# Strassen's scheme for the second product of experts 4 to 7 in the first super chunk, with half of the T blocks of w1 split beside the gated product

## The chip, the cores and the metric

The program runs on one core of one Trainium2 chip. The metric is the device time of one execution in microseconds, taken as the median of the runs shown. Times of single instructions and waits come from one profiled execution.

## The reference

Three layers follow one another. Only the third is touched by the change.

```python
x = attn_out.transpose(0, 2, 1, 3).reshape(2304, 512)       # linear attention, 32 heads
x = ((x @ w1) * (x @ w2) @ w3) @ w_out                       # gated product
def _moe2_ref(x, w_gate, w1, w2):                            # 8 experts, D = 512, F = 1024
    P = ...                                                  # 8 Sinkhorn rounds over x @ w_gate
    out = np.zeros((N, D), dtype=np.float32)
    for e in range(E):
        h = np.maximum(x @ w1[e], 0.0)                       # first product
        ye = h @ w2[e]                                       # second product
        out += P[:, e:e + 1] * ye
    return out
```

## The kernel before, in words

Every fp32 operand of a matmul is held as a high and a low part. `copy` makes the high part on ScalarE (a cast, line 96) and `subtract` the low part on VectorE (line 99). A product is then three matmuls (`mm3`, lines 87 to 89: high by high, low by high, high by low).

The gated product runs from about 235 to 558 us in six blocks `j` of 384 tokens, each with 16 accumulations `ab` and 4 accumulations `px`; `ab` has four PSUM banks. Beside it run 48 jobs (`sum_load`, `sum_make`, `sum_next`). Two of three jobs form the four sums T1 to T4 of a block of moe2_w1 that Strassen's scheme needs and store them to `W1T`. The third forms the sums of a block of moe2_w2 for one of the experts in `EARLY` (0, 1, 2 and 7), splits them with `copy` and `subtract` and stores high and low part to `W2S`. A job's tile `tr` has three buffers and its tile `tt` two. The load for job n+3 is issued by `sum_make(n)` and waits until the buffer is free.

The third layer has three super chunks `s` of 768 tokens. A super chunk runs over 8 experts `e`, each of 4 units `p`, and a unit `u` is (s, e, p). The first product of a unit (`products`) is by Strassen's scheme in all three super chunks: seven products of 384 columns on the operands a11, s2, s3, s1, a22, a12 and s4, each in one PSUM bank, which `c` then collects on VectorE (line 836). The weights of units 0 to 31 are loaded in fp32 (`load_w1`), split (`prep_w1`) and stored to `W1S`. Later super chunks load them from there (`back_w1`).

After four units comes the second product of the expert. In super chunk 0 it is a plain product of 512 columns, `py` at line 942, and `split_w2` and `sums_w2` prepare the parts of w2 that the later super chunks read. In super chunks 1 and 2 it is Strassen's scheme again: the PSUM pool has seven banks, `operands` makes the operands a, b, d and e from `c`, and seven groups of 36 matmuls of 256 columns (lines 1039 to 1041) multiply them with the blocks K11, K21, KT4, KT1, KN2, K22 and KT3 of w2, in this order. `load_t` loads these blocks from `W2S` into a ring `tk` of three buffers. A block is named t*s*_*e*_*k*, with k from 0 to 6.

Before the last second product of a super chunk, `load_x` loads the x of the next one (`rx`) and `prep_x` makes its seven operands with sums in a scratch tile `xs`, which is a tile of the pool `rx`. All DMAs named here are issued by SyncE (SP), in the order of the program, and a DMA that has to wait holds up all behind it. A scheduler sets the order on each engine, starting from the order of the code and its priorities.

Of the kernel before, what the change touches and what calls it, by code (L numbers as in the profile page):

```python
# [27 lines left out]
def kernel(  # L28
# [17 lines left out]
    nc = tc.nc  # L46
# [51 lines left out]
    def subtract(key, out, a, b, i=0):  # L98
# [11 lines left out]
        [scr.tile([P, 2, n, 2 * P], F32, name=f"w1s{i}_{n}") for n in (2, 5)]  # L110
        for i in range(NE * FT2 // 2)
    ]
    DH = DM // 2
    W2S = [scr.tile([P, 7, FT2 // 2, 2, DH], F32, name=f"w2s{i}") for i in range(NE)]

    W1T = [scr.tile([P, 4, 2 * P], F32, name=f"w1t{i}") for i in range(NE * FT2 // 2)]
# [363 lines left out]
    def prep_x(s):  # L480
# [3 lines left out]
        t = rx.tile([P, 2, N1], F32, name=f"xs{s}", tag="s")  # L484
# [22 lines left out]

    def load_w1(u):
        if u < len(units):
            s, e, p = units[u]  # L510
            if s > 0:
                return
            rawW1[u] = rw1.tile([P, 7, 2 * P], F32, name=f"r1_{u}", tag="r")
            nc.sync.dma_start(rawW1[u][:, 4:7], moe2_w1[e, p][:, 1:4])
            nc.sync.dma_start(rawW1[u][:, 0:4], W1T[u])
# [39 lines left out]
    EARLY = (0, 1, 2, NE - 1)  # L555

    def w2_rows(e, p):
        return moe2_w2[e].rearrange("(j n p) (h d) -> n p j h d", j=2, p=P, h=2)[p]

    def make_t(e, p, t, hi):  # L560
# [5 lines left out]
        lo = t.bitcast(F32R)  # L566
        copy("Th", hi, t)
        subtract("Tl", lo, t, f32(hi))
        for i, x in enumerate((hi, lo)):
            nc.sync.dma_start(W2S[e][:, 0:4, p, i], f32(x))  # L570

    first_jobs = [("w1", k) for k in range(len(W1T))]
# [13 lines left out]
    def sum_make(n):  # L586
        kind, k = jobs[n]
        t = tq[0].tile([P, 4, 2 * P], F32R if kind == "w2" else F32, name=f"tt{n}", tag="tt")
        if kind == "w2":
            make_t(*k, rawT[n], t)  # L590
            sum_load(n + 3)
            return
        b12, b11, b21, b22 = (rawT[n][:, i] for i in range(4))
        t1, t2, t3, t4 = (t[:, i] for i in range(4))
        add("Wt", t1, b12, b11, ALU.subtract, k)
        add("Wt", t3, b22, b12, ALU.subtract, k)
        add("Wt", t2, b22, t1, ALU.subtract, k)
        add("Wt", t4, b21, t2, ALU.subtract, k)
        sum_load(n + 3)
        nc.sync.dma_start(W1T[k], t)  # L600
# [10 lines left out]
    with ExitStack() as c2:  # L611
# [81 lines left out]
        for j in range(NT // N1):  # L693
# [26 lines left out]
            if c0 + N1 == NT:  # L720
# [5 lines left out]
                wc1 = sbuf(c4, "wc1", 2, "left")  # L726
# [40 lines left out]
    with c4:  # L767
# [24 lines left out]
        def split_w2(u):  # L792
# [10 lines left out]
            if e in EARLY:  # L803
                load_w2(u + len(RW))
# [353 lines left out]
```

## Time and profile before

| | |
|---|---|
| median of 3 runs | 2020.35 us (2019.73 to 2021.43) |
| the profiled execution | 2020.68 us, span of its instructions 2018.9 us |
| TensorE (PE) busy | 1987.1 us, 98% |
| VectorE (DVE) busy | 1426.9 us, 71% |
| ScalarE (ACT) busy | 779.6 us, 39% |
| granted TensorE clock | 0.995 of full speed over the span |
| DMA | 496.78 MB, 246 GB/s in the mean |

Each line gives an engine's busy time in the profiled execution. Super chunk 0 lies at 557.9 to 1064.5 us, super chunk 1 at 1064.5 to 1541, super chunk 2 after that.

### The profile page before, as it was taken

How to read it: one execution, taken by the hardware profiler on the slowest of the kernel's cores; microseconds unless marked ns; L12 is line 12 of the kernel's file. 1: busy time of each engine (PE TensorE's matmuls, PEld its weight loads, DVE VectorE, ACT ScalarE, POOL GpSimd, SP SyncE). 2: the span in 40 equal slices, each digit the busy share in tenths (PEclk: the TensorE clock that was granted, in tenths of full speed). 3: DMA queues.
4: the chain of work that ended last, by engine and by line, in shares of the span. 5: the costliest groups of instructions: out<-in, count | busy, mean ns of one | idle time of the engine just before them, and what ended most of it. 6: DMA issues, size and time to landing. Idle time of an engine off the chain costs nothing.

```text
span 2018.9 us, 33841 instructions
## 1 busy us (share of the span) xinstructions
PE 1987.1 (98%) x13605; PEld 1867.6 (93%) x13605; DVE 1426.9 (71%) x2454; ACT 779.6 (39%) x1435; POOL 92.4 (5%) x126
## 2 busy tenths in 40 slices
PE   7899999999999999999999999999999999999999
PEld 6676789999998888998889999999999999999999
DVE  7766775666687558877776766677778667786666
ACT  6666532323443224433333333334334333433333
POOL 3433200000000000000000000000000000000000
PEclk9999999999999999999999999999999999999999
DMA  6443247888597668989977677666778677666674
GB/s 213 146 140 108 90 151 255 275 294 283 197 342 286 245 250 303 330 315 317 326 269 277 237 252 255 246 247 248 251 250 307 243 246 252 249 250 248 243 253 152
DMA packets 155501, 496.78 MB, mean 246 GB/s; under 512 B 12624, under 2 KB 73936, under 8 KB 128464
## 3 DMA queue, kind: packets, MB, share of 16 engines
q1 hardware_dynamic: 154752, 493.96, 69.3%
q8 instruction: 107, 1.75, 0.4%
q10 hardware_dynamic: 592, 0.66, 0.1%
q14 instruction: 50, 0.41, 0.1%
HBM read 348.82 MB, written 145.75 MB: 245 GB/s over the span
## 4 chain that ended last, share of the span: by engine, by line
PE 87%; DVE 5%; ACT 3%; POOL 2%; DMA 2%; issue 1%; SPq 0%; ACTq 0%; POOLq 0%; DVEq 0%
PE ps L87 6%; PE ps L89 6%; PE ps L88 6%; PE pa L87 5%; PE pa L89 5%; PE pa L88 5%; PE py L89 4%; PE py L88 4%; PE py L87 4%; PE b L1041 3%; PE b L1040 3%; PE b L1039 3%; PE ab L89 3%; PE ab L87 3%; PE ab L88 3%; PE a L1039 2%
## 5 line engine op out<-in xcount | busy, mean ns | idle before, releaser
L836 DVE TENSOR_TENSOR c<-c,ps 128x384 f32<-128x384 f32 x480 | 255.9, 549 | 58.5 <-PE ps L89 54.2
L834 ACT COPY c<-pa 128x384 f32<-128x384 f32 x96 | 45.7, 476 | 321.0 <-PE pa L89 278.4
L89 PE MATMUL py<-w,hL 128*128 128x512 f32 x384 | 152.1, 397 | 0.0
L88 PE MATMUL py<-w,hH 128*128 128x512 f32 x384 | 152.0, 397 | 0.0
L87 PE MATMUL py<-w,hH 128*128 128x512 f32 x384 | 151.2, 397 | 0.0
L1058 DVE SCALAR_TENSOR_TENSOR o<-mt,Pw,o 128x512 f32<-128x512 f32 x84 | 58.4, 749 | 122.5 <-ACT mt L1048 122.5
L89 PE MATMUL ab<-XH,wL 128*128 128x384 f32 x384 | 131.1, 341 | 1.4 <-DVE wL L99 1.4
L87 PE MATMUL ab<-XH,wH 128*128 128x384 f32 x384 | 131.0, 341 | 1.2 <-ACT wH L96 1.0
L88 PE MATMUL ab<-XL,wH 128*128 128x384 f32 x384 | 130.4, 339 | 0.0
L836 DVE TENSOR_TENSOR c<-c,pa 128x384 f32<-128x384 f32 x192 | 103.0, 549 | 10.0 <-PE pa L89 9.0
L1039 PE MATMUL b<-t,dh 128*128 128x256 f32 x384 | 108.7, 283 | 0.0
L1040 PE MATMUL b<-t,dh 128*128 128x256 f32 x384 | 108.7, 283 | 0.0
L1041 PE MATMUL b<-t,dl 128*128 128x256 f32 x384 | 108.7, 283 | 0.0
L958 DVE SCALAR_TENSOR_TENSOR o<-py,Pw,o 128x512 f32<-128x512 f32 x42 | 31.5, 750 | 109.1 <-PE py L89 108.8
L993 ACT ACTIVATE c<-c 128x384 f32<-128x384 f32 x64 | 33.7, 526 | 155.6 <-DVE c L836 155.6
L96 ACT CAST w<-r 128x1024 fp32r<-128x1024 f32 (+2 forms) x96 | 63.8, 690 | 71.7 <-PE pa L89 27.1
L87 PEld LDWEIGHTS py<-w,hH 128*128 128x128 f32 x384 | 72.3, 188 | 17.4 <-DVE o L958 0.3
L89 PEld LDWEIGHTS py<-w,hL 128*128 128x128 f32 x384 | 72.3, 188 | 17.3
L88 PEld LDWEIGHTS py<-w,hH 128*128 128x128 f32 x384 | 72.4, 188 | 17.1
L87 PEld LDWEIGHTS ab<-XH,wH 128*128 128x128 f32 x384 | 72.6, 189 | 2.9 <-ACT wH L96 1.3
L99 DVE TENSOR_TENSOR w<-r,w 128x512 fp32r<-128x512 f32 (+2 forms) x96 | 72.5, 774 | 3.2 <-ACT w L96 3.0
L89 PEld LDWEIGHTS ab<-XH,wL 128*128 128x128 f32 x384 | 72.5, 189 | 2.1 <-DVE wL L99 2.1
(259 smaller groups left out, 6306.1 us busy)
## 6 DMA issues: line engine op xcount, KB each, us to landing
t<-w2s SPq DMA_DIRECT2D x112, 1024.0 KB, 4.8
w<-w1s SPq DMA_DIRECT2D x64, 1280.0 KB, 5.5
w1s<-w SPq DMA_DIRECT2D x32, 1280.0 KB, 7.1
w<-w1s SPq DMA_DIRECT2D x64, 512.0 KB, 5.0
tr<-in_moe_w_dram SPq DMA_DIRECT2D x48, 512.0 KB, 5.2
w2s<-w SPq DMA_DIRECT2D x96, 256.0 KB, 4.3
w1t<-tt SPq DMA_DIRECT2D x32, 512.0 KB, 6.4
r<-w1t SPq DMA_DIRECT2D x32, 512.0 KB, 6.8
```

The lines of the kernel that those rows point to most:

```text
L87: nc.tensor.matmul(ps, aH, bH, start=start, stop=False)
L88: nc.tensor.matmul(ps, aH, bL, start=False, stop=False)
L89: return nc.tensor.matmul(ps, aL, bH, start=False, stop=stop).ins
L96: (e.copy if e is nc.scalar else e.tensor_copy)(out, src)
L99: engine(key, i).tensor_tensor(out, a, b, ALU.subtract)
L834: first[0] = nc.scalar.copy(o, ps).ins
L836: nc.vector.tensor_tensor(o, t, ps, ALU.add)
L993: nc.scalar.activation(c22, c22, AF.Relu)
L1039: nc.tensor.matmul(dst[i], H[:, c], T[:, 0], start=f, stop=False, skip_group_check=True)
L1040: nc.tensor.matmul(dst[i], H[:, c], T[:, 1], start=False, stop=False, skip_group_check=True)
L1041: nc.tensor.matmul(dst[i], L[:, c], T[:, 0], start=False, stop=l, skip_group_check=True)
L1058: nc.vector.scalar_tensor_tensor(o, src[i], w, o, ALU.mult, ALU.add)
```

## The change

Experts 4 to 7 of super chunk 0 (units 16 to 31; `NUC` is 16) now take the path of the later super chunks: `operands`, `load_t` and the seven groups. Experts 0 to 3 stay as they were. `EARLY` is now experts 4 to 7, so that the jobs beside the gated product prepare the sums of w2 for these, and `sums_w2` prepares those of experts 0 to 3 within super chunk 0. For experts 4 to 7 of super chunk 0 `load_t` reads the plain blocks K11, K21 and K22 in fp32 through a tile `kr` with one buffer, splits them and stores them to `W2S`.

The jobs that form T1 to T4 of w1 for units 16 to 31 now split them too and store high and low part to `W1S`. For these units `get_w1` loads the T blocks from `W1S` and splits only B11, B21 and B22, which come through a tile `rwb` with one buffer. The parts of a unit are held as four T and three B blocks (before: five and two).

The scratch tile `xs` of `prep_x` is now a tile of the ring `tk`, for super chunk 0 one of its own.

```diff
+    EARLY = range(NE // 2, NE)
+    NUC = EARLY[0] * NP
...
+    def get_w1(u, i):
+        if u >= len(units):
             return
+        t = wc1.tile([P, 2, 4 - i, 2 * P], F32R, name=f"w1_{u}_{i}", tag=f"hl{i}")
+        WC.setdefault(u, []).append(t)
+        if u >= NU or i == 0 and u >= NUC:
+            nc.sync.dma_start(f32(t), W1S[u % NU][i])
+            return
+        r = rawW1[u] if u >= NUC else rawW1[u][:, 4 * i : 4 + 3 * i]
+        copy("Wh", t[:, 0], r)
+        subtract("Wl", t[:, 1], r, f32(t[:, 0]))
+        if i == 1 and u != NUC - 1:
+            load_w1(u + 1 if u >= NUC else u + 2)
+        nc.sync.dma_start(W1S[u][i], f32(t))
...
+    def store_t(dst, t, hi):
+        lo = t.bitcast(F32R)
+        copy("Th", hi, t)
+        subtract("Tl", lo, t, f32(hi))
+        for i, x in enumerate((hi, lo)):
+            nc.sync.dma_start(dst[i], f32(x))
...
+        if k < NUC:
+            nc.sync.dma_start(W1T[k], hi)
+        else:
+            store_t([W1S[k][0][:, i] for i in range(2)], t, hi)
...
         def load_t(u, k):
             s, e, p = units[u]
-            TK[k] = tk.tile([P, NP, 2, DH], F32R, name=f"t{s}_{e}_{k}", tag="t")
-            nc.sync.dma_start(f32(TK[k]), W2S[e][:, WK[k]])
+            t = TK[k] = tk.tile([P, NP, 2, DH], F32R, name=f"t{s}_{e}_{k}", tag="t")
+            if s > 0 or k not in KB:
+                nc.sync.dma_start(f32(t), W2S[e][:, WK[k]])
+                return
+            r = kr.tile([P, NP, DH], F32, name=f"k{e}_{k}", tag="k")
+            j, h = KB[k]
+            w = moe2_w2[e].rearrange("(j n p) (h d) -> j h p n d", j=2, p=P, h=2)[j, h]
+            nc.sync.dma_start(r, w)
+            copy("W2h", t[:, :, 0], r)
+            subtract("W2l", t[:, :, 1], r, f32(t[:, :, 0]))
+            nc.sync.dma_start(W2S[e][:, WK[k]], f32(t))
...
         for u, (s, e, p) in enumerate(units):
-            if s == 0:
+            if u < NUC:
                 continue
             operands(u)
...
-                prep_x(s + 1)
+                t = tk.tile([P, NP, 2, DH], F32, name=f"xs{s + 1}", tag="t")
+                t = t.rearrange("p n a d -> p (n a d)")[:, 0 : 2 * N1]
+                prep_x(s + 1, t.rearrange("p (a n) -> p a n", a=2))
```

At the turn from super chunk 1 to 2, SP's queue held these rows before. `rx2_0` and `rx2_1` are the two halves of the next x, and `t1_7_3` to `t1_7_6` the blocks KT1, KN2, K22 and KT3 of expert 7:

```order
L974 DMA t1_7_3_15144<-w2s7_156 128x2048
L477 DMA rx2_0_15064<-xs2_84 128x1536
L477 DMA rx2_1_15065<-xs2_84 128x1536
L974 DMA t1_7_4_15185<-w2s7_156 128x2048
L974 DMA t1_7_5_15223<-w2s7_156 128x2048
L974 DMA t1_7_6_15264<-w2s7_156 128x2048
```

With the change the same stretch of SP's queue reads:

```order
L476 DMA rx2_0_15784<-xs2_84 128x1536
L476 DMA rx2_1_15785<-xs2_84 128x1536
L966 DMA t1_7_3_15864<-w2s7_172 128x2048
L966 DMA t1_7_4_15905<-w2s7_172 128x2048
L966 DMA t1_7_5_15943<-w2s7_172 128x2048
L966 DMA t1_7_6_15984<-w2s7_172 128x2048
```

The load of `t1_7_3` has moved behind both loads of x. Not seen in these rows: the scratch `xs2` now takes the buffer after `t1_7_2` in the ring, so that `t1_7_5`, three tiles later, waits for the last reader of `xs2`. This is the instruction that makes `s4l2`.

On VectorE, in the last unit (19) of expert 4 of super chunk 0, stood these rows before. `hL` are the low parts of the operands of the plain second product:

```order
L836 TENSOR_TENSOR c19_8452<-c19_8452,ps219_8461 128x384
L99 TENSOR_TENSOR w2_18_8433<-r2b_6084,w2_18_8433 128x2x512
L836 TENSOR_TENSOR c19_8452<-c19_8452,ps319_8469 128x384
L99 TENSOR_TENSOR w1_20_5_8443<-r1_20_8358,w1_20_5_8443 128x1024
L836 TENSOR_TENSOR c19_8452<-c19_8452,ps119_8477 128x384 x2
L836 TENSOR_TENSOR c19_8452<-c19_8452,pa2219_8486 128x384
L836 TENSOR_TENSOR c19_8452<-c19_8452,pa1219_8494 128x384
L836 TENSOR_TENSOR c19_8452<-c19_8452,ps419_8504 128x384
```

With the change VectorE has these rows ahead of the same collecting of unit 19:

```order
L99 TENSOR_TENSOR w1_20_1_8582<-r1_20_8491,w1_20_1_8582 128x768
L1001 SCALAR_TENSOR_TENSOR c17_8422<-c17_8422 128x384
L99 TENSOR_TENSOR t0_4_1_8510<-k4_1_8511,t0_4_1_8510 128x4x256
L985 TENSOR_TENSOR dl17_8503<-c17_8422,dh17_8502 128x768
L985 TENSOR_TENSOR el17_8507<-c17_8422,eh17_8506 128x768
L982 SCALAR_TENSOR_TENSOR bl18_8589<-c18_8516,bh18_8588 128x768
L99 TENSOR_TENSOR w1_21_1_8672<-r1_21_8585,w1_21_1_8672 128x768
L836 TENSOR_TENSOR c19_8606<-c19_8606,ps219_8615 128x384
L998 TENSOR_TENSOR c18_8516<-c18_8516 128x384
L836 TENSOR_TENSOR c19_8606<-c19_8606,ps319_8623 128x384
L836 TENSOR_TENSOR c19_8606<-c19_8606,pa1219_8650 128x384
L836 TENSOR_TENSOR c19_8606<-c19_8606,ps119_8631 128x384 x2
```

The Strassen operands of units 17 and 18 (`dl`, `el`, `bl`) now stand there, as in the later super chunks, and with them what those do not have: the splits of w1's B blocks (`w1_20_1`, `w1_21_1`) and of a plain block of w2 (`t0_4_1`). Over the first product of an expert these are four splits of w1 (128x768) and two of w2 (128x4x256); the third of w2 falls into the second product.

In the gated product SP's queue held these rows before, of jobs 36 to 40:

```order
L600 DMA w1t24_181<-tt36_5211 128x1024
L582 DMA tr40_5255<-in_moe2_w1_dram 128x1024
L600 DMA w1t25_182<-tt37_5250 128x1024
```

With the change it holds for jobs 36 to 40:

```order
L558 DMA w1s24_4_133<-tt36_5219 128x1024
L558 DMA w1s24_4_133<-tr36_5102 128x1024
L592 DMA tr38_5186<-in_moe2_w2_dram 128x2x512
L558 DMA w1s25_4_135<-tt37_5261 128x1024
L590 DMA tr39_5228<-in_moe2_w1_dram 128x1024
L558 DMA w1s25_4_135<-tr37_5144 128x1024
```

Each job of w1 from unit 16 on has two stores, and the second one reads `tr`, so that the load that takes this buffer waits until it has landed.

## Rows read from the trace of the kernel before

**Rows 1.** Page, part 1: busy time, share of the span, instructions.
```profile
PE 1987.1 (98%) x13605; PEld 1867.6 (93%) x13605; DVE 1426.9 (71%) x2454; ACT 779.6 (39%) x1435; POOL 92.4 (5%) x126
```

**Rows 2.** Waits by engine and line after 245 us: total, times, longest.
```profile
PE px L87 <- DVE woH L96: 1.2, 1, 1.2
...
PE a L1039 <- DMA t<-w2s: 0.4, 1, 0.4
```

**Rows 3.** Windows: length, busy PE, PEld, DVE, ACT (POOL), granted clock, DMA share, GB/s.
```profile
904.78:938.51 33.73, 33.73 (x146) 27.12 (x145) 21.30 (x36) 7.77 (x9) 0.00 (x0) 1.00 0.99 339
1390.48:1420.70 30.22, 30.22 (x253) 30.22 (x253) 17.34 (x27) 8.87 (x20) 0.00 (x0) 1.00 0.75 262
1361.36:1390.48 29.12, 29.12 (x170) 29.12 (x169) 25.22 (x47) 12.27 (x21) 0.00 (x0) 1.00 0.65 234
```

**Rows 4.** Timeline of SP at the turn s = 1 to 2: start, length of issue.
```profile
1514.99 0.32 SPq L974 DMA_DIRECT2D t<-w2s  x1
...
1519.90 17.37 SPq L974 DMA_DIRECT2D t<-w2s  x5
```

**Rows 5.** Timeline of VectorE at this turn.
```profile
1518.55 0.95 DVE L985 TENSOR_TENSOR dl<-c,dh 128x768 fp32r<-128x768 f32 x1
...
1531.24 0.75 DVE L1058 SCALAR_TENSOR_TENSOR o<-mt,Pw,o 128x512 f32<-128x512 f32 x1
...
1534.30 1.41 DVE L1058 SCALAR_TENSOR_TENSOR o<-mt,Pw,o 128x512 f32<-128x512 f32 x2
1535.63 0.95 DVE L99 TENSOR_TENSOR s4l<-xs,s4h 128x768 fp32r<-128x768 f32 x1
```

**Rows 6.** Timeline of PE at this turn.
```profile
1522.12 0.28 PE L1039 MATMUL b<-t,dh 128*128 128x256 f32 x1
...
1526.43 0.34 PE L87 MATMUL pa<-a11h,w 128*128 128x384 f32 x1
...
1528.03 0.39 PE L1039 MATMUL a<-t,eh 128*128 128x256 f32 x1 [0.38 <-DMA t<-w2s]
```

**Rows 7.** Chain that ended last, its one step at this turn: start, length.
```profile
1519.90 8.08 DMA t<-w2s
```

**Rows 8.** DMA issues: count, KB each, median us to landing.
```profile
t<-w2s SPq DMA_DIRECT2D x112, 1024.0 KB, 4.8
...
w2s<-tr SPq DMA_DIRECT2D x16, 512.0 KB, 3.5
```

**Rows 9.** Windows at idle stretches of PE, columns as in rows 3.
```profile
18.80:20.60 1.80, 0.12 (x4) 0.09 (x2) 1.80 (x3) 0.97 (x4) 0.23 (x1) 1.00 0.84 288
20.90:24.30 3.40, 3.40 (x40) 2.93 (x37) 3.37 (x6) 2.23 (x4) 1.28 (x1) 0.50 0.92 345
...
224.50:226.20 1.70, 0.07 (x4) 0.01 (x2) 1.63 (x4) 1.70 (x5) 0.00 (x0) 1.00 0.08 24
226.20:233.00 6.80, 6.41 (x98) 4.08 (x102) 5.09 (x10) 5.40 (x16) 0.74 (x4) 1.00 0.50 155
```

**Rows 10.** Groups by line and form: total, mean ns of one, idle before.
```profile
L99 DVE TENSOR_TENSOR w<-r,w 128x1024 fp32r<-128x1024 f32 x32 | 39.0, 1219 | 0.4 <-ACT w L96 0.4
L985 DVE TENSOR_TENSOR el<-c,eh 128x768 fp32r<-128x768 f32 x64 | 61.0, 953 | 5.0 <-ACT eh L984 5.0
L96 ACT CAST w<-r 128x1024 fp32r<-128x1024 f32 x32 | 33.7, 1052 | 31.9 <-issue 11.5 <-PE pa L89 11.0 <-DVE c L836 5.0
```

**Rows 11.** Timeline of VectorE after the first product that ends at 1390.48.
```profile
1392.20 0.55 DVE L836 TENSOR_TENSOR c<-c,ps 128x384 f32<-128x384 f32 x1
```

**Rows 12.** Windows in the gated product and at its end, columns as in rows 3.
```profile
451.43:501.86 50.43, 50.43 (x290) 50.43 (x289) 31.59 (x68) 15.71 (x28) 0.00 (x0) 1.00 0.84 292
501.86:557.90 56.04, 55.69 (x323) 53.30 (x322) 34.23 (x61) 23.11 (x41) 0.00 (x0) 1.00 0.58 201
```

**Rows 13.** Timeline of VectorE before super chunk 0.
```profile
553.55 1.22 DVE L99 TENSOR_TENSOR w<-r,w 128x1024 fp32r<-128x1024 f32 x1
...
556.55 1.00 DVE L680 COPY lgs<-lg 16x384 f32<-16x384 f32 x2
```

More of the change, by code (lines that the diff above doesn't have):

```diff
@@ L109 @@
     W1S = [
-        [scr.tile([P, 2, n, 2 * P], F32, name=f"w1s{i}_{n}") for n in (2, 5)]
+        [scr.tile([P, 2, n, 2 * P], F32, name=f"w1s{i}_{n}") for n in (4, 3)]
         for i in range(NE * FT2 // 2)
@@ L113 @@
     DH = DM // 2
+    W1T = [scr.tile([P, 4, 2 * P], F32, name=f"w1t{i}") for i in range(NE * FT2 // 4)]
     W2S = [scr.tile([P, 7, FT2 // 2, 2, DH], F32, name=f"w2s{i}") for i in range(NE)]
-    W1T = [scr.tile([P, 4, 2 * P], F32, name=f"w1t{i}") for i in range(NE * FT2 // 2)]
     NPR = NPR_ALL // B
@@ L505, in prep_x @@
         split("a22", a22)
+    NU = len(W1S)
+    EARLY = range(NE // 2, NE)
+    NUC = EARLY[0] * NP
+    T3, T1, T4, T2, B11, B21, B22 = range(7)
     def load_w1(u):
-        if u < len(units):
+        if u < NU:
             s, e, p = units[u]
[L511 to L515, printed above, removed]
@@ L565, in make_t, with make_t1 @@
         add("Tw", b21, b21, b22, ALU.add)
[L566 to L572, printed above, removed]
+        store_t([W2S[e][:, 0:4, p, i] for i in range(2)], t, hi)
+    def make_t1(k, t, hi):
+        b12, b11, b21, b22 = (t[:, i] for i in range(4))
+        t3, t1, t4, t2 = (x[:, i] for x in (hi if k < NUC else t,) for i in range(4))
+        add("Wt", t1, b12, b11, ALU.subtract)
+        add("Wt", t3, b22, b12, ALU.subtract)
+        add("Wt", t2, b22, t1, ALU.subtract)
+        add("Wt", t4, b21, t2, ALU.subtract)
+        if k < NUC:
+            nc.sync.dma_start(W1T[k], hi)
+        else:
+            store_t([W1S[k][0][:, i] for i in range(2)], t, hi)
+    first_jobs = [("w1", k) for k in range(NU)]
     jobs = []
@@ L587, in sum_make @@
         kind, k = jobs[n]
-        t = tq[0].tile([P, 4, 2 * P], F32R if kind == "w2" else F32, name=f"tt{n}", tag="tt")
+        split = kind == "w2" or k >= NUC
+        hi = tq[0].tile([P, 4, 2 * P], F32R if split else F32, name=f"tt{n}", tag="tt")
         if kind == "w2":
[L590 to L598, printed above, removed]
+            make_t(*k, rawT[n], hi)
+        else:
+            make_t1(k, rawT[n], hi)
         sum_load(n + 3)
-        nc.sync.dma_start(W1T[k], t)
     made = [0]
@@ L726 @@
                 wc1 = sbuf(c4, "wc1", 2, "left")
+                rwb = sbuf(c4, "rwb", side="left")
                 c6 = c4.enter_context(ExitStack())
                 rw1 = sbuf(c6, "rw1", 2, "left")
-                wc1c = []
                 load_w1(0)
                 load_w1(1)
-                prep_x(0)
-                prep_w1(0)
+                prep_x(0, sbuf(c2, "xs0").tile([P, 2, N1], F32, name="xs0"))
+                for k in range(4):
+                    get_w1(*divmod(k, 2))
             for dt in range(KT):
@@ L912 @@
             load_w2(u)
-        NU = len(W1S)
-        for u, (s, e, p) in enumerate(units[:NU]):
-            if u + 1 < NU:
-                load_w1(u + 2)
-                prep_w1(u + 1)
-            if u + 2 == NU:
-                c6.close()
+        for u, (s, e, p) in enumerate(units[:NUC]):
             unit(u, between)
@@ L922 @@
                 split_w2(u)
-            if p == 0 and e > 0 and e - 1 not in EARLY:
+            if p == 0 and e > 0:
                 sums_w2(u - 1)
-            if e == NE - 1 and p == 1:
-                load_x(s + 1)
             if p < NP - 1:
                 continue
-            if e == NE - 1:
-                prep_x(s + 1)
             for tt in range(2 * N1 // P):
@@ L944 @@
                         between(behind)
-                if e not in EARLY and tt % 2:
+                if tt % 2:
                     sums_w2(u - NP + 1 + tt // 2)
```

49 lines of the change are left out of this document (14 added, 35 removed).

## The prediction

> **What bounds the kernel now.** I read the page first, then the waits, then windows by stage, and last the timelines of the two places where SP's queue changes. TensorE is busy for 98% of the span [rows 1]. The waits after 245 us say the same: the longest is 1.2 us, and the only one in the Strassen part is 0.4 us for a block of w2 [rows 2]. So the kernel is bound by TensorE, and a change gains what it takes from TensorE's work and loses every wait that it puts there. In the windows the reader is to see three prices: the plain second product of one expert takes 33.73 us, Strassen's takes 30.22 us, and the first product ahead of it 29.12 us, all with TensorE busy throughout at the full clock [rows 3]. VectorE beside the first product is at 25.22 of 29.12 us, which is not far from full.
>
> A turn is the last second product of a super chunk, with the loads of the next x beside it. Before, only one wait of 0.38 us stands in the turn from super chunk 1 to 2 [rows 6].
>
> **The gain.** Four second products go from 33.73 to 30.22 us: 4 x 3.51 = 14.04 us [rows 3]. The first products and the number of their matmuls stay. **-14.0 us**, if no wait comes in.
>
> **The turn from super chunk 1 to 2.** Two things move. First, the load of KT1 (`t1_7_3`). It was issued at 1514.99, ahead of x [rows 4]. Now it stands behind `rx2_1`, which waits until `dl` of the last unit, started at 1518.55, has freed its buffer [rows 5], so it goes out where the next block did, at 1519.90. That block took 8.08 us to land [rows 7], against a median of 4.8 us for such loads [rows 8]. So KT1 lands between 1524.7 and 1528.0; I take 1526.8, nearer to the row of this very place, where x is on its way too. TensorE wants it at 1522.12 [rows 6] plus the six matmuls of the next unit, which now stand ahead of KT1's group and not behind it, some 1.1 us: 1523.2. That is a wait of 3.6 us (1.5 to 4.8). Second, the load of K22 (`t1_7_5`) now waits for the last reader of `xs2`, `s4l`. That began at 1535.63 [rows 5]. Three `o` additions, 0.75 and 1.41 us, which stood between the sums and `s4l`, now stand behind it, so I put its end at 1534.5 (1533.9 to 1536.6). Plus 4.8 us [rows 8] K22 lands at 1539.3. Before, K22's group began one group after 1528.03 [rows 6], a seventh of 30.22 us later, at 1532.35. So the rest of the second product is late by 7.0 us, and KT1's wait is inside that, since two groups after 1526.8 TensorE is done at 1535.4 and waits again for 3.9 us. I take a little off, because x no longer shares the DMA engines with a block issued just ahead: **+6.5 us** (5 to 8).
>
> **The turn from super chunk 0 to 1.** It has the same order now, with one difference: K22 of this super chunk is read in fp32 into `kr` early, and only its cast (1052 ns) and subtract (1219 ns) [rows 10] come behind `s4l`, 2.3 us in place of 4.8 us. The same sum gives 7.0 - 2.5 = 4.5 us, and KT1's wait of 3.6 us is again inside it: **+4.5 us** (3 to 6).
>
> **The clock after these waits.** [...] What follows the first wait of a turn is hidden in the second, which a landing ends. [...] I take **+2.0 us**, nearer to the row without a fall, because TensorE is full on both sides of these waits.
>
> [...]
>
> **VectorE in experts 4 to 7.** The first product of each now has what super chunk 1 has, 25.22 us [rows 3], and besides four splits of w1's B blocks of the size of `el`, 953 ns, and two of w2's blocks at 1219 ns [rows 10]: 25.22 + 3.81 + 2.44 = 31.5 us in 29.12 us. It does not fit. The excess is 2.3 us for each expert. It first goes into the lag that VectorE may have: the last product is collected at 1392.20, 1.7 us after TensorE was done with it at 1390.48 [rows 11, 3], without a wait of TensorE, since seven banks are there. The second product has room again (17.34 of 30.22 us), so the lag does not grow from one expert to the next. Bounds: 0, if the banks take it all, and 4 x 2.3 = 9.4 us, if they take nothing. Following the order of VectorE and ScalarE row by row, I find the cast of the next B blocks ahead of a collecting copy in ScalarE's order in units 19 and 27, which holds a bank. I take a little over half of the excess: **+5.0 us** (0 to 9.4).
>
> **The jobs beside the gated product.** Sixteen of them get a cast (1052 ns), a subtract (1219 ns) [rows 10] and a second store of 512 KB. In the block at 451.43 VectorE is at 31.59 of 50.43 us and the DMA engines at 0.84 with 292 GB/s [rows 12]. In the order of the change this block holds ten jobs in place of twelve, and two more go to the last one. Ten jobs of three times 512 KB are 15.7 MB, 312 GB/s in 50.43 us, and the plain second product reaches 339 GB/s [rows 3]; VectorE comes to some 38 us. A job has 5.0 us, and its longest chain, a store (3.5 us [rows 8]) and the load that it holds back, must be hidden by three `tr` buffers. I take **+0.5 us** (0 to 6).
>
> **The start of super chunk 0.** Unit 1's weights are now split ahead of it. Before, the chain there ran through VectorE: the split at 553.55 and then the logits' copies `lgs`, which end at 557.55 [rows 13], just before the first product. The last block of the gated product has VectorE at 34.23 of 56.04 us [rows 12], so two more jobs and two more splits fit, but `XL`, which the logits read, comes later. **+0.6 us** (0 to 3).
>
> **Sum.** -14.0 + 6.5 + 4.5 + 2.0 + 5.0 + 0.5 + 0.6 = +5.1 us (+0.25%). The profiled span is 2018.9 us, the profiled execution 2020.68 us, 0.33 us over the median of 2020.35 us. I add the sum to the median: **2025.4 us**.
>
> **Rivals.**
> - *VectorE has more room than its busy time says (faster).* Its instructions overlap a little, and both the collecting in experts 4 to 7 and the sums of x at the turns hang on it. If it keeps up, the term of 5.0 us is 0, the turns are at their lower bounds (5 + 3), and their waits are short enough for a full clock, as at 224.5: -14.0 + 8 + 0.5 + 0.6 = -4.9 us, 2015.4 us. For it speaks the lag of 1.7 us without a wait. Against it speak the 31.5 us in 29.12 and the chain through `s4l`, which is long without VectorE being late. It decides when turns and experts together cost under 9 us.
> - *Break-even.* The turns cost what they should (11.0), the clock does not fall and the banks take nearly all of VectorE's excess: -14.0 + 11.0 + 1.0 + 1.1 = -0.9 us, 2019.5 us. What speaks for it is that a turn's terms follow from the order alone.
> [...]
> - *The jobs become the bound.* If store and reload take a job to 5.7 us in place of 5.0, a block of ten is 6 to 7 us late, VectorE's fixed order holds the four `ab` banks, and TensorE waits there: 2031 to 2034 us. The DMA share of 0.84 before speaks for it, the rate of 339 GB/s elsewhere against it.
>
> **Chances and range.** About 0.2%, 4 us, is what a measurement here can tell from no change: faster is below 2016.3, slower above 2024.4 us. Forecast (2024 to 2029) 0.37, VectorE's room 0.18, break-even 0.31, clock 0.07, jobs 0.07. Faster 0.18; same 0.33, break-even and the forecast's lower edge; slower 0.49. The range goes from 2014.0, beyond the faster rival, to 2031.5, which takes in the clock's and half of the jobs'. It leaves out some 0.15.
>
> **What would show it.** In the changed trace: second products of experts 4 to 7 of 30.2 us; at both turns a wait of TensorE on `t` by DMA before KT1's group and at the turn from 1 to 2 another before K22's, together 5 to 8 us there; the granted clock below 1 in the windows behind them; waits of TensorE on VectorE's or ScalarE's `c` at the starts of the second products of experts 4 to 7, 1 to 2 us each; none over 1 us between 245 and 557 us. The prediction is wrong if the turns show no waits, so that the blocks landed earlier than these rows let me think, or if TensorE's waits in experts 4 to 7 are below 1 us in all or above 9.

## The result and the profile after

The change makes the kernel slower by nearly three times what was forecast, 14.5 us in place of 5.1: 2035.95 us (median of 5 runs, 2034.32 to 2044.84) against 2021.43 us (5 runs, 2019.73 to 2021.71), a ratio of 1.0084 with a 95% interval of 1.0067 to 1.0100. The forecast was 2025.4 us, and the range ended at 2031.5 us. The profiled execution took 2034.95 us with a span of 2033.2 us, 14.3 us more than that of before.

The waits of TensorE after 245 us, by engine and line (total, times, longest), answer to [rows 2]:

```profile
PE b L1041 <- DMA t<-w2s: 8.3, 4, 3.3
PE a L1041 <- ACT c L834: 5.3, 4, 2.5
PE pa L87 <- ACT a11h L96: 1.8, 1, 1.8
PE px L87 <- ACT cH L718: 1.8, 2, 1.1
...
PE px L88 <- DVE cL L719: 1.0, 1, 1.0
```

TensorE waits for the blocks of w2 (`t`) and for the collecting copy `c`, as the prediction's steps had it, and for the last operands of `px` (`cH`, `cL`), where it foresaw no wait over 1 us. The next fence has windows of the changed kernel: the `px` accumulations of blocks 4 and 5 of the gated product, the start of expert 6's second product, and then the two turns in pieces. Columns as in [rows 3].

```profile
484.77:503.17 18.40, 17.18 (x97) 16.61 (x97) 12.39 (x24) 7.99 (x13) 0.00 (x0) 1.00 0.94 315
536.97:557.49 20.52, 18.78 (x97) 18.12 (x97) 19.05 (x25) 12.98 (x20) 0.00 (x0) 0.92 0.85 288
...
971.07:990.07 19.00, 19.00 (x135) 19.00 (x136) 14.16 (x25) 7.83 (x15) 0.00 (x0) 0.93 0.90 347
...
1047.39:1052.37 4.98, 1.92 (x6) 1.16 (x6) 3.40 (x4) 3.07 (x6) 0.00 (x0) 0.66 1.02 430
1052.37:1071.25 18.88, 18.88 (x145) 18.88 (x145) 15.09 (x20) 5.78 (x11) 0.00 (x0) 0.91 0.66 231
...
1528.31:1532.86 4.55, 1.21 (x8) 0.89 (x6) 2.46 (x3) 3.06 (x6) 0.00 (x0) 1.00 1.03 429
1532.86:1554.13 21.27, 19.09 (x145) 18.92 (x145) 13.96 (x19) 4.74 (x10) 0.00 (x0) 0.92 0.58 212
```

Whole stages, in the same columns: experts 4 to 7 up to the last second product, and the two turns.

```profile
817.04:1032.34 215.30, 209.73 (x1430) 208.01 (x1428) 174.09 (x283) 96.34 (x165) 0.00 (x0) 0.99 0.80 291
1032.34:1071.25 38.91, 34.01 (x259) 33.04 (x259) 30.27 (x43) 16.15 (x29) 0.00 (x0) 0.91 0.78 284
1515.37:1554.13 38.76, 33.24 (x260) 32.75 (x259) 27.25 (x38) 14.73 (x28) 0.00 (x0) 0.96 0.66 242
```

A turn without waits is 30.22 us and six matmuls of 1.1 us, 31.3 us, so they are 7.6 and 7.5 us too long. The experts should have taken 4 x 29.12 + 3 x 30.22 = 207.1 us [rows 3] and took 8.2 us more. The `px` windows are 1.8 and 3.9 us over the 16.64 us that they take without a wait (rows of e3 below). The reader is also to see the clock column: four stretches are at 0.91 to 0.93 and one at 0.66, each behind waits or with waits in it.

What the turn from super chunk 1 to 2 looks like can be read row by row against [rows 4] to [rows 6]. SP's DMA queue in the changed kernel:

```profile
1520.34 5.69 SPq L476 DMA_DIRECT2D rx<-xs  x2
1526.07 17.53 SPq L966 DMA_DIRECT2D t<-w2s  x5
```

VectorE's row of `s4l`:

```profile
1539.46 0.96 DVE L99 TENSOR_TENSOR s4l<-xs,s4h 128x768 fp32r<-128x768 f32 x1 [0.90 <-ACT s4h L96]
```

And TensorE's, at the first matmuls of KT1's and of K22's group:

```profile
1532.86 0.39 PE L1041 MATMUL b<-t,dh 128*128 128x256 f32 x1 [3.34 <-DMA t<-w2s]
...
1545.42 0.36 PE L1041 MATMUL b<-t,dh 128*128 128x256 f32 x1 [2.17 <-DMA t<-w2s]
```

The second product began at 1515.37. KT1's load goes out 10.7 us later, behind x, and its group starts at 17.5 us (foreseen: 17.6, from 1509.18 to 1526.8). `s4l` ends at 1540.42, and K22's group starts 5.0 us after that, 30.1 us after the start (foreseen: 30.1). The times of this step were right to about a tenth of a us. The 0.5 us that the prediction then took off, for less traffic, did not come.

### The profile page after: what moved, and what is told of

Read it like the earlier page. It is cut to its first block, busy times and chain, and to the rows that moved or that the text cites. A ratio compares the mean times of both kernels' runs of the same rounds, so it can differ in the third digit from the quotient of the medians.

```text
span 2033.2 us, 34889 instructions
## 1 busy us (share of the span) xinstructions
PE 1976.7 (97%) x14037; PEld 1879.5 (92%) x14037; DVE 1487.9 (73%) x2538; ACT 821.5 (40%) x1511; POOL 92.7 (5%) x126
## 4 chain that ended last, share of the span: by engine, by line
PE 75%; DVE 10%; DMA 7%; ACT 4%; issue 2%; POOL 2%; SPq 0%; ACTq 0%; POOLq 0%; DVEq 0%
PE ps L87 6%; PE ps L89 6%; PE ps L88 6%; PE pa L87 4%; PE pa L88 4%; PE pa L89 4%; PE b L1041 4%; PE b L1043 4%; PE b L1042 4%; PE a L1041 3%; PE a L1042 3%; PE a L1043 3%; PE py L88 2%; PE py L89 2%; PE py L87 2%
## 5 line engine op out<-in xcount | busy, mean ns | idle before, releaser
L1041 PE MATMUL b<-t,dh 128*128 128x256 f32 x480 | 137.7, 287 | 8.3 <-DMA t<-w2s 8.3
L1042 PE MATMUL b<-t,dh 128*128 128x256 f32 x480 | 137.1, 286 | 0.0
L1041 PEld LDWEIGHTS b<-t,dh 128*128 128x128 f32 x480 | 93.6, 195 | 9.6 <-DMA t<-w2s 7.3
L1042 PEld LDWEIGHTS b<-t,dh 128*128 128x128 f32 x480 | 93.6, 195 | 0.0
L1043 PEld LDWEIGHTS b<-t,dl 128*128 128x128 f32 x480 | 93.5, 195 | 0.0
L1043 PE MATMUL a<-t,el 128*128 128x256 f32 x320 | 90.6, 283 | 0.0
L1042 PE MATMUL a<-t,eh 128*128 128x256 f32 x320 | 90.6, 283 | 0.0
L1041 PE MATMUL a<-t,eh 128*128 128x256 f32 x320 | 90.5, 283 | 0.0
L984 ACT CAST eh<-c 128x768 fp32r<-128x768 f32 x80 | 66.6, 833 | 51.7 <-DVE c L1000 51.7
L982 DVE SCALAR_TENSOR_TENSOR bl<-c,bh 128x768 fp32r<-128x768 f32 x80 | 76.1, 952 | 8.1 <-ACT bh L981 8.1
L985 DVE TENSOR_TENSOR el<-c,eh 128x768 fp32r<-128x768 f32 x80 | 76.2, 952 | 6.2 <-ACT eh L984 6.2
L985 DVE TENSOR_TENSOR dl<-c,dh 128x768 fp32r<-128x768 f32 x80 | 76.0, 950 | 1.7 <-ACT dh L984 1.7
L88 PE MATMUL py<-w,hH 128*128 128x512 f32 x192 | 76.2, 397 | 0.0
```

The source lines that it names most:

```text
L88: nc.tensor.matmul(ps, aH, bL, start=False, stop=False)
L982: nc.vector.scalar_tensor_tensor(lo, src, 0.0, f32(hi), ALU.max, ALU.subtract)
L984: nc.scalar.copy(hi, src)
L985: nc.vector.tensor_tensor(lo, src, f32(hi), ALU.subtract)
L1041: nc.tensor.matmul(dst[i], H[:, c], T[:, 0], start=f, stop=False, skip_group_check=True)
L1042: nc.tensor.matmul(dst[i], H[:, c], T[:, 1], start=False, stop=False, skip_group_check=True)
```

## The experiments

**e1: the scratch of x out of the ring.**

```diff
-                t = tk.tile([P, NP, 2, DH], F32, name=f"xs{s + 1}", tag="t")
-                t = t.rearrange("p n a d -> p (n a d)")[:, 0 : 2 * N1]
+                t = rwb.tile([P, 3, 2 * P], F32, name=f"xs{s + 1}", tag="r")
+                t = t.rearrange("p n d -> p (n d)")
```

> The scratch of the x sums for super chunks 1 and 2 lies in the free tile of w1's B blocks in place of the ring of w2's blocks; all else as changed. Theory A (the waits at the two turns come from this scratch in the ring: KT1's load behind x, K22's load behind the last sum): TensorE's waits on t by DMA, 8.3 us in all, fall below 1 us, the granted clock stays at 1.00 behind both turns, each turn loses 6 to 8 us, and the time is 2020 to 2024 us. Rival B (the blocks land late because the DMA engines carry more, at 430 GB/s there): waits of 2 us or more on t stay at both turns, and the time is 2029 us or more.

Measured: 2026.85 us (7 runs, 2021.38 to 2028.56), 1.0028 of before (1.0017 to 1.0039). With the scratch elsewhere the scheduler also put KT1's load ahead of x again. The waits on `t` fall from 8.3 to 1.1 us, the turns take 33.4 and 32.3 us, 12 us less together. Theory A holds for the turns; what the scratch cost by itself and what the order of the two loads cost, e1 does not tell apart. The median did not fall to 2024 us. The profiled execution, at 2023.63 us, did, although `px` lost more in it: super chunk 0 starts at 565.4 in place of 562.75, with nothing edited in the gated product. What lengthens the other executions, no profile shows. Windows of e1, `px` of blocks 4 and 5, and the turn from 1 to 2:

```profile
484.19:505.40 21.21, 18.62 (x98) 18.03 (x97) 14.42 (x28) 8.39 (x13) 0.00 (x0) 0.92 0.91 310
539.19:560.13 20.94, 18.55 (x98) 17.89 (x98) 19.13 (x25) 13.64 (x22) 0.00 (x0) 0.92 0.86 295
1509.86:1542.20 32.34, 31.51 (x259) 31.19 (x259) 26.39 (x38) 14.53 (x28) 0.00 (x0) 1.00 0.79 297
```

Block 4 is at a clock of 0.92 here, with a wait for `cH` of 2.46 us at 490.44, and was at 1.00 in the changed kernel, where the wait at this place (489.64) was 1.07 us. The length of the wait alone does not decide: in e5 below it is 3.07 us and the clock 1.00. That the clock is the cause of e1's spread, 2021.38 to 2028.56 us, is not shown.

**e2: the splits of experts 4 to 7 on GpSimd.**

```diff
-        copy("Wh", t[:, 0], r)
-        subtract("Wl", t[:, 1], r, f32(t[:, 0]))
+        copy("Wh" if u < NUC else "Bh", t[:, 0], r)
+        subtract("Wl" if u < NUC else "Bl", t[:, 1], r, f32(t[:, 0]))
...
-            copy("W2h", t[:, :, 0], r)
-            subtract("W2l", t[:, :, 1], r, f32(t[:, :, 0]))
+            copy("Kh", t[:, :, 0], r)
+            subtract("Kl", t[:, :, 1], r, f32(t[:, :, 0]))
```

> The splits of w1's B blocks and of w2's plain blocks in experts 4 to 7 of super chunk 0 (cast and subtract) go to GpSimd in place of ScalarE and VectorE; all else as changed. Theory A (VectorE and ScalarE are too full there, and the last collecting copy stands behind a cast): the four waits of the second products on ScalarE's c, 5.3 us, fall below 1 us, the clock stays full after expert 6's, and the time falls by 5 to 8 us, to 2028 to 2031 us. Rival C (the order of ScalarE's queue is not the cause, or GpSimd beside VectorE slows VectorE's instructions): the waits stay above 3 us, or move to w, and the time stays within 3 us of 2036.

Measured: 2053.87 us (4 runs), 1.0164 of before (1.0148 to 1.0180), 18 us slower than the change. `Bh`, `Bl`, `Kh` and `Kl` are set to GpSimd. The waits on `c` rose to 12.9 us. The rows of GpSimd's subtracts and of VectorE's `bl`, the low part of the operand b, in the first product of expert 4 of e2 show why:

```profile
837.96 0.94 DVE L982 SCALAR_TENSOR_TENSOR bl<-c,bh 128x768 fp32r<-128x768 f32 x1
...
845.25 2.56 POOL L99 TENSOR_TENSOR t<-k,t 128x1024 fp32r<-128x1024 f32 x1
845.51 3.13 DVE L982 SCALAR_TENSOR_TENSOR bl<-c,bh 128x768 fp32r<-128x768 f32 x1
```

`bl` takes 951 ns on average in this stretch of the changed kernel. In e2 it takes 3.13 us and, at 826.62, 2.27 us where it overlaps a subtract of GpSimd, and 0.94 us where it overlaps none. Rival C was right that the move does not help, and the reason is the second one that it gave; its time, within 3 us of 2036, was not right. What makes `bl` longer beside a subtract of GpSimd, no run shows.

**e3: jobs without their split.** The jobs of units 16 to 31 store the sums twice without cast and subtract, so the low parts of these T blocks are missing. The sums are made in `tt`, and both stores read `tt`; in the changed kernel the second store reads `tr`.

```diff
-        t3, t1, t4, t2 = (x[:, i] for x in (hi if k < NUC else t,) for i in range(4))
+        t3, t1, t4, t2 = (x[:, i] for x in (hi,) for i in range(4))
...
-            store_t([W1S[k][0][:, i] for i in range(2)], t, hi)
+            for i in range(2):
+                nc.sync.dma_start(W1S[k][0][:, i], hi)
...
-        split = kind == "w2" or k >= NUC
+        split = kind == "w2"
```

> The jobs of units 16 to 31 store the T sums twice and leave out their cast and subtract, so the T blocks of these units have no proper low part in all three super chunks; DMA traffic is as changed. Theory A (the casts and subtracts make VectorE and ScalarE late for the px accumulations of blocks 4 and 5): the waits on cH and cL, 2.8 us, go, the clock stays full in the last block, and super chunk 0 starts at 558 to 559 us in place of 562.75, the time falls by 4 us. Rival D (the second store and the load that it holds back make the jobs late): super chunk 0 still starts at 561 us or later.

Measured: 2031.29 us (2 runs), 1.0058 of before. The waits on `cH` and `cL` are gone, super chunk 0 starts at 559.2 in place of 562.75, and the last `px` window is

```profile
537.35:553.99 16.64, 16.64 (x97) 16.56 (x97) 14.70 (x17) 11.60 (x18) 0.00 (x0) 1.00 0.79 273
```

So the loss in `px` comes from the splits in the jobs; by the start of super chunk 0 it is theory A. But the edit takes away two things at once: the cast and the subtract, and the store that holds `tr` and with it the load that takes this buffer. The waits of VectorE from 440 to 556 us (and, with SPq, of SP's queue), in the kernel before, in the changed kernel and in e3:

```profile
DVE a L715 <- PE ab L89: 15.6, 10, 2.5
...
DVE tr L468 <- DMA tr<-in_moe_w_dram: 0.5, 1, 0.5
```

```profile
SPq L590 <- DMA w1s<-tr: 20.3, 12, 3.1
...
DVE tr L99 <- ACT tt L96: 17.3, 17, 2.8
DVE tr L467 <- DMA tr<-in_moe_w_dram: 10.1, 13, 2.0
```

```profile
DVE a L718 <- PE ab L89: 15.6, 11, 2.6
...
DVE tr L467 <- DMA tr<-in_moe_w_dram: 3.1, 2, 2.1
```

In the changed kernel VectorE never gets ahead of TensorE's `ab` here. Against the kernel before it has twelve more subtracts of 1.22 us (19 in place of 7), waits 8.6 us longer for casts (8.7 before), and 9.6 us longer for loads of `tr`, which SP's queue holds until a store from `tr` has landed. Which of the three is needed for the loss, e3 does not tell. How the lateness reaches TensorE, the order on VectorE at the end of block 5 of the changed kernel shows:

```profile
538.17 1.80 DVE L467 TENSOR_TENSOR tr<-tr 128x256 f32<-128x256 f32 x4
539.89 0.55 DVE L717 TENSOR_TENSOR a<-ab,a 128x384 f32<-128x384 f32 x1
540.35 0.95 DVE L467 TENSOR_TENSOR xs<-rx 128x768 f32<-128x768 f32 x1
541.22 1.22 DVE L99 TENSOR_TENSOR tr<-tr,tt 128x1024 fp32r<-128x1024 f32 x1
542.35 0.55 DVE L719 TENSOR_TENSOR cL<-a,cH 128x384 fp32r<-128x384 f32 x1
```

TensorE was done with the last `ab` at 536.97. The product `a` comes 2.9 us later, behind the sums of the last job, and `cL` behind that job's subtract.

**e4: filled waits.**

```diff
+            fill(24)
             group(KT1, b1)
...
+            with tc.issue_after(last[0]):
+                fill(16)
...
             group(K22, b1)
```

> 24 and 16 more matmuls of 256 columns, into a bank that nobody reads, stand in the two waits of TensorE at the turn from super chunk 1 to 2; nothing else differs. They take some 2.9 and 1.9 us of waits of 3.3 and 2.2 us. Theory A (part of the turn's cost is the clock that falls after these waits): the landings stay, the granted clock in the stretch behind the first wait is 1.00 in place of 0.92, and the turn is shorter by 1 to 2 us. Rival (the lower clock has another cause, or costs nothing): the stretch is as long as before, within 0.3 us.

`last[0]` is the last matmul of KN2's group. Measured: 2030.65 us (2 runs), 1.0054 of before; the turn takes 36.45 us in place of 38.76. But the expectation's "nothing else differs" did not hold: K22's load went out at 1534.49 there, before `s4l` was done, into another buffer of the ring, so the shorter turn is not the clock's alone. What can be compared are the 72 matmuls of KT1 and KN2, in the changed kernel first and in e4 second:

```profile
1532.86:1543.25 10.39, 10.38 (x72) 10.18 (x72) 8.58 (x11) 4.13 (x9) 0.00 (x0) 0.84 0.29 102
```

```profile
1529.88:1538.61 8.73, 8.73 (x72) 8.73 (x73) 7.76 (x10) 3.97 (x8) 0.00 (x0) 1.00 0.59 215
```

With the wait filled the granted clock is 1.00 in place of 0.84, and the same work takes 1.66 us less. In the changed kernel TensorE then waited 2.17 us for K22 anyway, so at this turn the slow stretch cost nothing: it only shortened that wait. For the total the experiment is inconclusive.

**e5: cast and subtract of B behind the collecting copy** (on top of e1).

```diff
             product("s4", B22, (c12, c12))
-            get_w1(u + 2, 1)
+            with tc.issue_after(first[0]):
+                get_w1(u + 2, 1)
```

> As e1, and the cast and subtract of the B blocks of unit u+2 stand behind the copy that collects the first product of unit u, and so behind the collecting on VectorE too; nothing else differs. Theory A (the order is what holds the banks: the cast waits for the last product of the unit or for its load, with the copy queued behind it): the four waits of the second products on ScalarE's c, 4.5 us in e1, fall below 1 us, and so does the stretch at half clock behind expert 6's, so the time is 5 to 7 us below e1, at 2019.5 to 2022 us. Rival C (VectorE does not get its work done in these first products, whatever the order): waits of the same size on VectorE's c or on operands take their place, and the time is within 2 us of e1's 2026.85.

Measured: 2021.72 us (12 runs, 2015.93 to 2026.78), 1.0009 of before (0.9999 to 1.0018), 5.1 us below e1 in the medians. The profiles can't carry this difference: e5's shows an execution of 2026.63 us, 3.0 us more than e1's, because `px` lost more again. What they show is that the waits on `c` fall from 4.5 to 2.5 us, the longest is 1.0 in place of 2.4 us, and the granted clock over experts 4 to 7 is 1.00 (822.77 to 1033.72 us). So neither theory's mark was met: the waits are not below 1 us, and not of the same size. With the old order (e1, e3, e4, e6) these waits come to 4.4 to 4.8 us, with the new one to 2.4 to 2.6 us (e5, e7, e8), in e12 to 4.0 us. In the changed kernel ScalarE's rows had read

```profile
847.12 0.83 ACT L96 CAST w<-r 128x768 fp32r<-128x768 f32 x1 [2.07 <-PE ps L89]
847.85 0.47 ACT L834 COPY c<-pa 128x384 f32<-128x384 f32 x1
```

ScalarE idles for 2.07 us at a cast that, by the profile, waits for the last product of the unit, while the copy behind it holds the bank that the second product wants. In e5 the copy comes first and waits for VectorE, which is the lateness that stays:

```profile
852.25 0.48 ACT L834 COPY c<-pa 128x384 f32<-128x384 f32 x1 [1.97 <-DVE el L986]
```

**e6: split jobs first** (on top of e1). **e7: e1, e5 and e6 together.**

```diff
-    first_jobs = [("w1", k) for k in range(NU)]
+    first_jobs = [("w1", k % NU) for k in range(NUC, NUC + NU)]
```

> As e1, and the jobs of w1 begin with units 16 to 31, which are split, and end with units 0 to 15; the work of the jobs is the same. Theory A (the split jobs make VectorE late at the ends of blocks 4 and 5, since there are six of them in the last block): two or three jobs less crowd there, the waits of px on cH and cL, 4.8 us in e1, fall below 1.5 us, super chunk 0 starts 4 to 8 us earlier (565.4 in e1), and the time is 4 to 8 us below e1, at 2019 to 2023 us. Rival D (the sum of the work decides): px waits as long in blocks 2 and 3, and the time is within 2 us of e1.

> e1, e5 and e6 together: scratch apart, cast behind copy, split jobs first. Theory A (the three losses are independent of each other, and each falls away with its cause): what is left of the change's loss against the kernel before is about 2 us at the start of super chunk 0 and 1.5 us of waits at the turns and in the experts, and the gain of 14 us stands: 2008 to 2013 us. Rival (the losses share the room of VectorE, so that one comes back where another goes): 2015 us or more.

Measured: e6 2025.09 us (9 runs), 1.0027 (1.0017 to 1.0037); e7 2021.97 us (11 runs), 1.0009 (1.0000 to 1.0017). In both profiles block 5 is clean, and the lateness has moved forward. The longest of e7's waits from 245 to 560 us:

```profile
PE lg L679 <- ACT XH L748: 4.8, 2, 2.8
```

These are the logits behind blocks 1 and 2, which the split jobs now meet. For e6 theory A has the waits of `px` right and the start of super chunk 0 wrong (563.0, 2.3 us earlier in place of 4 to 8); the time is rival D's, 1.8 us below e1: the lateness moved, to the logits and not to `px`. For e7 theory A, with independent losses, lies 9 us below the result, and its rival holds.

**e8: e5 with jobs without their split** (as e3, the low parts of these T blocks are missing).

> As e5 (scratch apart, cast behind copy), and the jobs of units 16 to 31 store the T sums twice and leave out their cast and subtract, so the T blocks of these units have no proper low part in all three super chunks. Theory A (what is left of the loss in e5 comes from VectorE and ScalarE beside the gated product, by waits of px and the half clock behind them): super chunk 0 starts at 558 to 560 us, 8 us earlier than in e5's profile, and the time is 2009 to 2014 us. Rival D (it is the second store and the reload of the jobs, or the experts themselves): 2018 us or more.

Measured: 2014.89 us (9 runs, 2010.65 to 2019.07), 0.9971 of before (0.9962 to 0.9981), 6.8 us below e5. The last `px` windows of e8 first, of e5 second:

```profile
487.45:504.09 16.64, 16.64 (x98) 16.64 (x98) 8.84 (x20) 4.61 (x7) 0.00 (x0) 1.00 1.01 365
537.88:554.52 16.64, 16.64 (x97) 16.56 (x97) 14.70 (x18) 11.59 (x18) 0.00 (x0) 1.00 0.80 274
```

```profile
486.51:506.99 20.48, 17.26 (x97) 16.56 (x97) 15.19 (x28) 8.49 (x13) 0.00 (x0) 1.00 0.95 331
540.79:563.22 22.43, 19.94 (x97) 19.28 (x97) 19.84 (x26) 13.82 (x22) 0.00 (x0) 0.85 0.85 287
```

This is theory A, 0.9 us above its range, with super chunk 0 at 559.8 us: with the turns and the order mended, the splits of sixteen jobs cost some 7 us. As in e3, the store that holds `tr` is gone too. The bytes are not the cause: the DMA engines are at 365 GB/s in the first window and TensorE is busy throughout. Of the 14.0 us of gain 5.5 us are left even so.

**e9 to e11: Strassen's scheme in experts 6 and 7 only**, on top of e5, with eight split jobs in three places and unit 1 split after the logits.

```diff
-    NUC = EARLY[0] * NP
+    NUC = 24
...
-    first_jobs = [("w1", k) for k in range(NU)]
+    first_jobs = [("w1", k) for k in [*range(24, 32), *range(24)]]                     # e9: first
+    first_jobs = [("w1", k) for k in [*range(16), *range(24, 32), *range(16, 24)]]     # e10: block 3
+    first_jobs = [("w1", k) for k in [*range(8), 24, 8, 25, 9, 26, 10, ...]]           # e11: spread
```

> Scratch apart and cast behind copy as in e5, but only experts 6 and 7 of super chunk 0 by Strassen's scheme (units 24 to 31), so that only eight jobs of w1 split their T blocks; these come first among the jobs, and unit 1's weights are split after the logits. The gain is halved to 7.0 us. Theory A (the jobs' splits late in the gated product cost most of what e5 loses, at full size 7 to 10 us, and early they are caught up by the lighter jobs): super chunk 0 starts within 1.5 us of the kernel before, experts 6 and 7 and the turns cost 2 to 3 us, and the time is 3 to 5 us below before, at 2015.5 to 2017.5 us. Rival (loss and gain both scale with the experts): no change, 2019.5 to 2021.5 us.

> As e9 (experts 6 and 7 only, scratch apart, cast behind copy), but the eight split jobs lie in block 3 of the gated product, where no logits are computed between the blocks, and not in block 1. Theory A (a split job costs only where it meets a deadline: the logits of blocks 0 to 2, or the ends of blocks 4 and 5): the wait of 3.1 us of the logits on XH in e9 and its half clock go, super chunk 0 starts within 1.5 us of the kernel before, and the time is 3 to 5 us below before: 2015.5 to 2017.5 us. Rival (the splits cost what they cost in any block): 2019 us or more.

> As e10, but the eight split jobs are spread: one in each group of three jobs from job 12 to 34, with a plain job of w1 and a job of w2 between them. Theory A (a split job makes the jobs late by some half a us each, and plain jobs between them catch up): the wait of px on cH at the end of block 4, 3.0 us in e10, falls below 1 us, super chunk 0 starts within 1.5 us of the kernel before, and the time is 3 to 5 us below before: 2015.5 to 2017.5 us. Rival (the lateness of the jobs adds up over the gated product, however they are spread): waits of 2 us or more at the ends of blocks or at the logits, and 2019 us or more.

Measured: e9 2023.59 us, 1.0013 (1.0004 to 1.0022); e10 2021.77 us, 1.0002 (0.9993 to 1.0011); e11 2018.10 us, 0.9994 (0.9985 to 1.0003), 11 runs each. In a row, e9 waits 3.1 us for the logits' `XH` (350.00 to 354.00 us then at a clock of 0.71), e10 3.0 us for `cH` at the end of block 4, and e11 for neither. e9 is above both of its ranges, e10 in its rival's, e11 between the two. But e10 did not do what it was to do: block 4 starts at 452.9 us, and four of the eight split jobs of w1 store from `tr` behind that, from 456.09 on. The last of these stores and the wait at the block's end:

```profile
476.68 0.41 SPq L558 DMA_DIRECT2D w1s<-tr  x1
...
493.58 0.44 PE L87 MATMUL px<-cH,woH 128*128 128x384 f32 x1 [2.98 <-ACT cH L718]
```

So e10 is one more case of split jobs close together and a late end of a block; split jobs in block 3 alone were not tried, nor is it shown that lateness is carried from block to block. Spread, the jobs fit; `px` of blocks 4 and 5 in e11:

```profile
484.55:501.64 17.09, 16.94 (x98) 16.61 (x98) 11.14 (x24) 4.99 (x10) 0.00 (x0) 1.00 0.90 322
535.43:552.07 16.64, 16.64 (x98) 16.56 (x97) 13.78 (x17) 11.59 (x18) 0.00 (x0) 1.00 0.81 280
```

Super chunk 0 starts at 557.65 us, as before. Of the 7.0 us of gain the span shows 2.9 us; TensorE's waits behind 960 us come to 3.9 us, the longest 1.9 us for ScalarE's `mt` at the turn from 0 to 1.

**e12: all four experts with the sixteen split jobs spread**, on top of e5.

```diff
+    first_jobs = [("w1", k) for k in [k for i in range(16) for k in (16 + i, i)]]
```

> All four experts 4 to 7 as in the change, scratch apart, cast behind copy, unit 1 split after the logits, and the sixteen split jobs spread: one in each group of three from the first job to the last. Theory A (spread jobs are caught up by the plain ones between them, as in e11 with eight): the waits of px and of the logits stay under 2 us in all, super chunk 0 starts within 3 us of the kernel before, and the time is that of e8 within 4 us: 2012 to 2018 us. Rival (with a split job in every group of three nothing is left to catch up in): waits of 4 us or more beside the gated product, and 2019 to 2023 us, as in e5 and e7.

Measured: 2019.31 us (11 runs, 2014.76 to 2021.13), 0.9992 of before (0.9983 to 1.0001). Super chunk 0 starts 3.4 us later than before, some 2.4 us of it after block 1. The median lies in the rival's range, by 0.3 us, and the profile is nearer to theory A: `px` and the logits wait 1.9 us in all behind block 0. Experts 4 to 7 keep 4.0 us of waits on `c`. e11 and e12 are the best versions that compute the whole result; neither can be told from the kernel before.

## Why the prediction was wrong

The direction was right, and so were the places of the waits on `t` and on `c`; the size was not, and `px` was a place without a price. What each step cost, from the windows above (what the slow stretches cost is taken out of their stages and stands in a line of its own):

| step | foreseen, us | measured, us | from |
|---|---|---|---|
| gain of four second products | -14.0 | -14.0 | 30.2 us each without waits |
| turn 1 to 2 | +6.5 | +7.1 | 38.76 - 31.3, less 0.38 before |
| turn 0 to 1 | +4.5 | +7.3 | 38.91 - 31.3 - 0.34 clock |
| experts 4 to 7 | +5.0 | +6.9 | 215.30 - 207.1 - 1.3 clock |
| clock | +2.0 | +3.3 | 0.08 x 20.52; 0.07 x 19.0; 0.34 (see below) |
| jobs | +0.5 | +4.0 | 1.8 + 3.9 - 1.6 clock |
| start and all else | +0.6 | -0.3 | the rest of 14.3 |

*The jobs.* This is the step that failed most, +0.5 us foreseen and +4.0 measured: "Ten jobs ... VectorE comes to some 38 us ... I take +0.5 us (0 to 6)". The busy time was not the mistake: in block 4 (450.98 to 503.17 us) VectorE is busy for 35.8 us, less than foreseen, and the DMA engines move 308 GB/s. The step judged a block by its busy share and took a job's chain as hidden: "a store ... and the load that it holds back, must be hidden by three `tr` buffers". It was not: from 440 to 556 us VectorE waits 10.1 us for such loads and 17.3 us for casts (rows beside e3). A job's instructions stand between `a` and `cL` in a fixed order, and the last ones of a block meet a deadline: `px` needs all eight `cH` and `cL`. e3 and e8 showed that the loss goes when these jobs are not split; whether cast and subtract or the held-back load weighs more stays open. The rival on the jobs, with a chance of 0.07, named store and reload and came nearest in time (2031 to 2034 us); its wait of TensorE was to be at the `ab` banks and came at `px`. The sentence on the two jobs more in the last block ("two more go to the last one") named the place and gave it no price.

*The clock.* The +2.0 us were meant for the turns, and no run shows that term: in the changed kernel the slow stretches cost some 0.34 us at the turns, and 2.9 us in `px` of block 5 and in expert 6. Each turn has one slow stretch (1052.37 to 1055.60 us at 0.50, 1532.86 to 1543.25 us at 0.84), and what follows hides most of it, as the prediction said. At the turn from 1 to 2 it only shortens the wait for K22, and behind that wait of 2.17 us the granted clock stays at 1.00. At the turn from 0 to 1 it costs 1.61 us (18.88 less 17.27, four groups of 30.22 / 7), but K22 was ready only 0.34 us before TensorE came to it:

```profile
1061.04 1.23 DVE L99 TENSOR_TENSOR t<-k,t 128x1024 fp32r<-128x1024 f32 x1 [1.11 <-ACT t L96]
...
1062.61 0.28 PE L1041 MATMUL b<-t,dh 128*128 128x256 f32 x1
```

The subtract that makes K22's low part ends at 1062.27. Without the slow stretch TensorE would have come earlier and waited for it, so the stretch costs some 0.34 us, an estimate from these rows. What the step left out are the 1.6 us in `px` of block 5 and the 1.3 us in expert 6, behind waits of 0.74 and 1.00 us close together (541.5) and of 2.55 us (971.07, the clock at 0.50 up to 973.70), while none came behind 1.98 us (848.38). The two rows that the prediction chose between [rows 9] hardly differ, 1.80 and 1.70 us of window, and neither is a wait for a DMA: TensorE idles 1.68 us before 20.54 without a releaser in the profile, and 1.63 us before 226.19 for ScalarE's `e`. Of the three waits for a DMA of over 1 us at the turns one was followed by a slow stretch (3.34 us), one lay in a stretch that had begun before it (2.51 us), and one was not followed (2.17 us). The falls in `px` and in expert 6 come behind waits for ScalarE and VectorE.

*Experts 4 to 7.* Foreseen 5.0 us; the profile has 5.3 us of waits on `c`, at all four starts, and 0.25 us on `t`; the other 1.3 us no row shows as a wait. The mechanism on ScalarE that the prediction named is the one that e5 removed, some 2 of 4.5 us; the rest is VectorE's lateness.

*The turn from 0 to 1* was mis-sized because its chain starts later than at the turn from 1 to 2. x's loads wait for VectorE's `dl`, which starts 5.9 us after the second product in place of 4.0, and the first one took 7.3 us to land in place of 4.8. So KT1's load went out 12.7 us after the start, in place of 10.7, six matmuls waited 1.8 and 0.6 us for the split of x, and K22, whose lateness the 4.5 us were, was ready after 29.9 us (foreseen: 27.6). TensorE was itself so late that no wait for K22 shows.

*The range.* All mis-sized terms but the turn from 0 to 1 (7.3 us, bounds 3 to 6) and the clock, a single figure, lie within the bounds that their steps gave. The range did not reach the sum because it let the terms miss to both sides, and all of any size missed to the same side. That they have VectorE's lateness in common was argued for the faster rival and not for the slower one; e7 showed that a loss taken away in one place comes back in part in another.

## What to carry to other kernels

Busy share over a stage does not price added work on an engine with a fixed order: look for the next instruction behind it that the bounding engine waits for, and count what stands ahead of it there, waits for casts and loads included. A scratch tile put into a ring of prefetch buffers makes the prefetch wait for the scratch's last reader; a free tile elsewhere gave back 9 us in the medians (e1). Where several small terms hang on the same busy engine, add their bounds on one side for the range.

## What the runs showed of the hardware

How long TensorE waited does not alone tell whether the clock falls behind it. At the end of block 4 a wait of 2.46 us was followed by a slow stretch (e1, clock 0.92 over `px`) and one of 3.07 us was not (e5, 1.00). In the changed kernel one of 1.98 us at the start of expert 4's second product was not followed by one (848.38 to 861.44 us at 1.00), and two of 0.74 and 1.00 us close together in `px` of block 5 were (544.50 to 546.50 us at 0.50). In this `px` and in expert 6 a slow stretch was worth 1.6 and 1.3 us, an estimate from clock and length of the windows (0.08 x 20.52 and 0.07 x 19.0). e5, with waits for `cH` of 4.6 us, scatters from 2015.93 to 2026.78 us, against 2018.12 to 2022.48 us for the kernel before beside it; e8, with none, from 2010.65 to 2019.07 us. That the clock is the cause of the scatter was not tried. VectorE's `bl`, 951 ns in the changed kernel, took 2.27 and 3.13 us where a subtract on GpSimd ran beside it, and 0.94 us where none did (e2).
